# Two layers of linear attention and MLP on one core: the key weights in four loads, the last store on another queue, and new instruction orders

## The chip, the core and the metric

The kernel runs on one core of a Trainium2 chip. A core has five engines that run side by side, each through its own list of instructions in order: TensorE (PE in the profile; its weight loads are PEld), VectorE (DVE), ScalarE (ACT), GpSimd (POOL) and SyncE (SP). They meet through semaphores. DMAs are issued by an engine's sequencer (here SP, ScalarE and GpSimd) and move data while the engines work. The metric is the device time of one execution in microseconds; lower is better.

## What is computed

```python
def _A_ref(x, wqkv, wo):                      # linear attention, 32 heads of 16
    qkv = (x @ wqkv) ...                      # 2048 tokens, 512 -> 3 * 512
    phi = lambda t: jnp.where(t > 0, t + 1, jnp.exp(t)) + 1e-6
    pq, pk = phi(q), phi(k)
    kv = jnp.einsum("bhsd,bhse->bhde", pk, v)
    z = jnp.einsum("bhsd->bhd", pk)
    num = jnp.einsum("bhqd,bhde->bhqe", pq, kv)
    den = jnp.einsum("bhqd,bhd->bhq", pq, z)[..., None] + 1e-6
    return (num / den) ... @ wo

def _B_ref(x, w1, b1, w2, b2):                # MLP, 512 -> 1792 -> 512
    y = _layernorm(x, axis=-1)
    h = _gelu(jnp.einsum("bsd,df->bsf", y, w1) + b1)
    return jnp.einsum("bsf,fd->bsd", h, w2) + b2

x = A_x
x = x + _A_ref(_layernorm(x, axis=-1), A_wqkv, A_wo)
x = x + _B_ref(_layernorm(x, axis=-1), B_w1, B_b1, B_w2, B_b2)
x = x + _A_ref(_layernorm(x, axis=-1), A_wqkv, A_wo)
x = x + _B_ref(_layernorm(x, axis=-1), B_w1, B_b1, B_w2, B_b2)
```

Inputs and output are bf16; x has 2048 tokens of 512.

## The kernel before, in words

**Tiling.** The 2048 tokens are 16 tiles of 128 (st 0 to 15), four to a chunk (c 0 to 3). L is the layer, 0 or 1. Weights stay on the chip.

**The order is written out by hand.** `build_kernel` lists every operation with its engine, what it reads and writes, and the buffers it takes. `CONF["ORDER"]` gives, for each engine, the names of its operations in the order in which they run; `CONF["PLACES"]` the buffer slot of each tile; `CONF["WAY"]` which engine or method does an operation that several could do; `CONF["LOADS"]` the first loads, each with name, queue, tensor, chunk, first and last part, and what it is issued behind. Semaphore waits follow from these (`assign_waits`). No engine leaves its order, so an operation whose input is late holds up all that stands behind it on its engine.

**The start.** The loads are x0 (token tile 0 of chunk 0, 128 KB), x1 (tiles 1 to 3, 384 KB), wk0 and wk1 (key weights, parts 0 and 1, then 2 and 3, of four parts of the contraction, 256 KB each), xc1, xc2, xc3 (the other chunks of x, 512 KB each) and wq (query weights, 512 KB). Each tile is normalised: `stats` and `aggr` (L772, L774), `veps` (variance plus epsilon, L779), `pow` (L781, GpSimd), `norm` (L800 on DVE or L795 on ScalarE). The first two tiles are also centred only (`cen`, L786), so that their keys need not wait for the scale. The keys need the tokens transposed: tiles 0 to 3 by TensorE (`PTC`, `PTA0`, L822) with a copy by ScalarE (`tc`, L832); all others, and tiles 0 and 1 for the queries, by a DMA transpose on SP (`TA`, L809). `K0_st` (L876) are the four matmuls of a tile's keys, into one bank; `K0_0` is in two pieces, a (parts 2 and 3) and b (parts 0 and 1). `phi` follows: `exp` (L844) and `relu` (L855) on ScalarE, `min` (L857 or L848) and `phi` (L861 or L850) on DVE or GpSimd. Then `G` (keys by normalised tokens, L968, L997), `Q` (queries, L893, and L906 for chunk 0 of layer 0) and `Z` (sums of keys, L951). TensorE runs `warm` matmuls on constants (L746) until its first real input is there.

**Between the parts of a layer.** G is copied (`cpg`, L984 on DVE, L981 on ScalarE), `KV` (L1018) makes the value product, `kvm` (L1037, DVE) masks it, `M` (L1041) multiplies it by wo, and `cpm` copies the result into `gtb` (`cpm0_2` on DVE, L984; the other three on ScalarE, L981). `WO0_0_0` to `WO0_0_3` (L1107), one piece for each column of `gtb`, make the first tile's attention output. The denominators of chunks 1 to 3 are done by token: `pz` (L1061), `red` (L1064), `den`, `rec`, `pr` (L1073), then a DMA transpose on SP (`TP`, L1077).

**The MLP.** `W1` (L1137) with `gelu` (L1142), `W2` (L1174) with a residual add `RB` (L1180; in the last layer L1184, into a bf16 tile), `b2` (L1123) adds the bias ahead of it. `TB` are the DMA transposes of its normalised tokens. In the last layer each tile is stored by SP (`OD`, L1186).

**The end.** The last tile, 15, is done in two pieces: 384 columns (h0) and 128 columns (h1), each with its own matmuls (L1160), add (`RB1_15_0`, `RB1_15_1`, L1166) and store (`OD15_0`, `OD15_1`, L1168), both on SP. Tile 10 is the one before it on TensorE. SP's last orders are OD8, OD9, OD15_0, OD10, OD15_1; DVE's are RB1_9, RB1_8, RB1_15_0, RB1_10, RB1_15_1. SP waits for all stores at the end.

**attn_z.** It adds up the keys: in layer 0 by matmul with ones for each chunk (`Z0_c`); in layer 1 by adding tiles into `zacc` (`za`, DVE or GpSimd, L923) for the first three chunks, turned into sums by `ZH`, and by matmul for the fourth.

Of the kernel before, what the change touches and what calls it, by code (L numbers as in the profile page):

```python
# [1345 lines left out]
```

## Time and profile before

| what | value |
|---|---|
| median of 3 runs | 324.53 us (324.09 to 324.61) |
| the profiled execution | 324.26 us |
| its span, first to last instruction | 323.0 us |
| busy time of PE / DVE / ACT / POOL | 318.4 / 216.9 / 189.8 / 145.6 us |
| matmuls | 1703 |
| first real matmul (PTC0), first key matmul | 4.65, 5.81 us |
| last matmul ends (modelled) | 320.44 us |

The loads and first transposes, by issue and landing:

| load | queue | issued at (us) | landed at (us) |
|---|---|---|---|
| x0 | SP | 0.80 | 3.21 |
| x1 | SP | 1.25 | 4.33 |
| wk1 | ACT | 1.49 | 5.67 |
| wk0 | SP | 1.71 | 6.03 |
| xc1 | ACT | 3.23 | 7.42 |
| TA0_0 | SP | 5.54 | 8.04 |
| xc3 | SP | 6.89 | 10.55 |
| wq | SP | 7.50 | 11.97 |
| TA0_1 | SP | 9.00 | 12.61 |
| xc2 | SP | 10.24 | 14.50 |
| TA0_4 | SP | 11.80 | 14.99 |

A busy share near 100% on TensorE says that it is never long without an instruction, not that it runs at its best. Matmuls overlap, so the distance from one start to the next tells what a matmul costs in a row; the recorded duration (379 ns on average for 512 columns) is its whole passage. The busy shares of the span, in 40 slices:

```profile
PE   7999999999999999999999999999999999999996
DVE  6988799998886763027378999999868872101003
ACT  5898656696640628667782377888735333653320
POOL 6674598784427433303634215967835273000000
```

Each digit is the busy share of one slice in tenths. TensorE's row has two slices that are not 9, the first and the last.

### The profile page before, as it was taken

What the parts mean: (1) busy time and instruction counts of PE and PEld (TensorE: products, weight loads), DVE (VectorE), ACT (ScalarE), POOL (GpSimd) and SP (SyncE); (2) the same over time, 40 slices, a digit from 0 to 9 for tenths busy, and PEclk for the clock granted to TensorE, in tenths of its full rate; (3) what the DMA queues carried; (4) which work ended last, traced back from release to release, by engine and by line L of the source; (5) the groups of instructions that cost most, each with busy time, mean ns of one, the idle gap of its engine ahead of it and who ended that gap; (6) DMA issues with size and microseconds to landing.
All of it is one profiled execution on the core that took longest, in us unless ns stands there. A gap on an engine that the chain in (4) does not pass through costs nothing.

```text
span 323.0 us, 4748 instructions
## 1 busy us (share of the span) xinstructions
PE 318.4 (99%) x1703; PEld 157.5 (49%) x1703; DVE 216.9 (67%) x528; ACT 189.8 (59%) x324; POOL 145.6 (45%) x217
## 2 busy tenths in 40 slices
PE   7999999999999999999999999999999999999996
PEld 3444544666445444444444444558644444444443
DVE  6988799998886763027378999999868872101003
ACT  5898656696640628667782377888735333653320
POOL 6674598784427433303634215967835273000000
DMA  6843792332212413011101300132034222201002
GB/s 211 244 87 79 253 334 54 63 81 36 49 32 35 81 32 67 17 31 37 34 3 30 51 16 0 35 62 57 19 79 89 59 65 67 49 0 35 16 32 65
DMA packets 52323, 21.68 MB, mean 67 GB/s; under 512 B 47500, under 2 KB 50828, under 8 KB 52300
## 3 DMA queue, kind: packets, MB, share of 16 engines
q1 hardware_dynamic: 50828, 15.88, 22.7%
q0 software_dynamic: 1056, 4.72, 4.4%
q10 hardware_dynamic: 416, 0.79, 0.7%
q8 instruction: 13, 0.21, 0.3%
q14 instruction: 10, 0.08, 0.1%
...
## 4 chain that ended last, share of the span: by engine, by line
PE 92%; DVE 3%; POOL 2%; ACT 1%; DMA 1%; issue 0%
PE ps L1137 30%; PE ps L1174 29%; PE ps L876 9%; PE ps L1107 8%; PE ps L893 5%; PE ps L997 4%; PE ps L906 2%; PE ps L968 2%; DMA t<-in_A_x_dram 1%; POOL lr L1061 1%; POOL t L1092 1%; PE ps L1160 1%; PE ps L951 1%; POOL w L725 1%; DVE rd L1064 0%; DVE eb L848 0%
## 5 line engine op out<-in xcount | busy, mean ns | idle before, releaser
L1142 ACT ACTIVATE gT<-ps,b1c 128x512 bf16<-128x512 f32 (+1 forms) x140 | 76.8, 601 | 62.4 <-PE ps L1137 61.8
L1137 PE MATMUL ps<-t,w 128*128 128x512 bf16 (+1 forms) x560 | 102.7, 336 | 0.0
L1174 PE MATMUL ps<-w,gT 128*128 128x512 bf16 x434 | 98.2, 379 | 0.0
L1137 PEld LDWEIGHTS ps<-t,w 128*128 128x128 bf16 x560 | 54.8, 98 | 44.3 <-ACT gT L1142 0.4
L1174 PEld LDWEIGHTS ps<-w,gT 128*128 128x128 bf16 x434 | 42.5, 98 | 49.9
L844 ACT ACTIVATE eb<-ps 128x512 bf16<-128x512 f32 x62 | 36.1, 602 | 25.9 <-PE ps L876 10.9
L781 POOL TENSOR_TENSOR rstd<-veps,neghalf 128x1 f32<-128x1 f32 x64 | 38.1, 607 | 15.4 <-DVE veps L779 13.1
L1184 DVE TENSOR_TENSOR yb<-ps,xsb 128x512 bf16<-128x512 f32 x15 | 10.2, 685 | 43.9 <-PE ps L1174 43.9
L772 DVE BATCH_NORM_STATS2 stats<-xsb 128x6 f32<-128x512 f32 x48 | 32.2, 678 | 0.1
L1107 PE MATMUL ps<-gtb,t 128*128 128x512 bf16 x128 | 31.6, 379 | 0.4 <-DVE gtb L984 0.4
L876 PE MATMUL ps<-wqkv,t 128*128 128x512 bf16 x128 | 31.1, 379 | 0.6 <-ACT t L832 0.6
L795 ACT ACTIVATE yb<-xsb,nmr,rstd 128x512 bf16<-128x512 f32 x21 | 17.0, 815 | 20.0 <-POOL nmr L792 19.8
L855 ACT ACTIVATE rb<-ps 128x512 bf16<-128x512 f32 x43 | 25.3, 600 | 3.1 <-PE ps L893 2.1
L779 POOL TENSOR_SCALAR veps<-mv 128x1 f32<-128x1 f32 x36 | 10.6, 295 | 36.0 <-DVE mv L774 30.8
L1061 POOL TENSOR_TENSOR lr<-t,zrow 128x512 f32<-128x512 bf16 x17 | 20.1, 1182 | 10.7 <-DVE t L850 4.9
L893 PE MATMUL ps<-wqkv,t 128*128 128x512 bf16 x96 | 24.1, 379 | 0.0
L1123 POOL TENSOR_TENSOR xsb<-xsb,b2b 128x512 f32<-128x512 f32 x17 | 19.9, 1181 | 4.9 <-DVE yb L800 4.7
L1180 DVE TENSOR_TENSOR xsb<-ps,xsb 128x512 f32<-128x512 f32 x16 | 10.9, 688 | 15.6 <-PE ps L1174 15.5
L800 DVE TENSOR_SCALAR yb<-xsb,mv,rstd 128x512 bf16<-128x512 f32 x27 | 14.4, 533 | 9.7 <-POOL rstd L781 9.5
L1073 POOL TENSOR_TENSOR t<-t,rr 128x512 bf16<-128x512 bf16 x14 | 14.9, 1070 | 12.1 <-DVE rr L1069 10.9
L1107 PEld LDWEIGHTS ps<-gtb,t 128*128 128x128 bf16 x128 | 12.5, 98 | 15.1 <-DVE gtb L984 0.9
L876 PEld LDWEIGHTS ps<-wqkv,t 128*128 128x128 bf16 x128 | 12.2, 98 | 15.0 <-ACT t L832 1.0
(100 smaller groups left out, 364.7 us busy)
## 6 DMA issues: line engine op xcount, KB each, us to landing
...
t<-yb SPq DMA_TRANSPOSE x62, 2.5
...
```

Of the source, the lines that this page charges most:

```text
L772: G.op("dve", lambda e: e.bn_stats(stats[:, s.slot, :], src()), 620, reads=src_keys, writes=[k + "s"], tiles=[s, *src_tiles], name=f"stats ...
L781: G.op("pool", lambda e: e.tensor_tensor(rstd[:, s.slot:s.slot + 1], veps[:, s.slot:s.slot + 1], neghalf[:], op=ALU.pow), 570, reads=[k + ...
L844: G.op("act", lambda e: e.activation(eb[:, et.slot, :], bank(bt), ACT.Exp, scale=by()), 478, reads=[src_key, *more_keys], writes=[f"e{tag} ...
L855: G.op("act", lambda e: e.activation(rb[:, rt.slot, :], bank(bt), ACT.Relu, scale=by()), 478, reads=[src_key, *more_keys], writes=[f"r{tag ...
L876: ins = e.matmul(bank(b), lhsT=yTa(yT)[:, dt, k * P:(k + 1) * P], rhs=wqkv[:, dt, D:2 * D], start=(i == 0 and n == 0), stop=(i == len(part ...
L893: ins = e.matmul(bank(b), lhsT=yTa(yT)[:, dt, k * P:(k + 1) * P], rhs=wqkv[:, dt, 0:D], start=(dt == 0), stop=(dt == DT - 1))
L1061: lambda e, r=r, tok=tok: e.tensor_tensor(lr[:, r.slot, :], tok(), zrow[:], op=ALU.mult), 1150 if on_pool else 600,
L1107: ins = e.matmul(bank(wb), lhsT=yTa(pq)[:, kt, k * P:(k + 1) * P], rhs=gtb[:, kt, :], start=(kt == 0), stop=(kt == DT - 1))
L1123: G.op("pool" if on_pool else "dve", lambda e: e.tensor_tensor(xsb[:, st, :], xsb[:, st, :], b2b[:], op=ALU.add), 1120 if on_pool else 600 ...
L1137: ins = e.matmul(bank(b, n), lhsT=w1[:, dt, ft * P:(ft + 1) * P], rhs=yTa(yT)[:, dt, k0 * P:k1 * P], start=(dt == 0), stop=(dt == DT - 1))
L1142: G.op("act", lambda e, ft=ft, b=b, k0=k0, k1=k1, n=n: e.activation(gT[:, g.slot, ft * 512 + k0 * P:ft * 512 + k1 * P], bank(b, n), ACT.Ge ...
L1174: ins = e.matmul(bank(b), lhsT=gT[:, g.slot, ft * 512 + k * P:ft * 512 + (k + 1) * P], rhs=w2[:, ft, :], start=(ft == 0), stop=(ft == FT - 1))
```

## The change

**Loads.** The key weights come in four loads of one part each, 128 KB: wkb (part 2) and wkd (part 3) on ScalarE's queue, wka (part 0) and wkc (part 1) on SP's. xc1 moves from ScalarE's queue to SP's. SP now issues xc1, wq and xc3 ahead of the first transpose, TA0_0.

**The first tile's keys.** K0_0 is in four pieces, in the order of parts 2, 0, 3, 1, each reading its own load; PTC1 stands between the second and the third.

**The end.** RB1_10 and OD10 stand ahead of RB1_15_0 and OD15_0. OD15_1 is issued by ScalarE.

**Orders.** All five orders are new. By place, 359 of 387 entries of TensorE's differ, 489 of 528 of DVE's, 191 of 310 of ScalarE's, 201 of 213 of GpSimd's and 100 of 112 of SP's. 435 of 705 tiles have another slot. 43 small operations change between DVE and GpSimd: 22 go to DVE, 21 to GpSimd. The set switches of ScalarE's table stay 14.

**attn_z** is rewritten so that the chunks of layer 0 that are added by `za`-like operations could be listed under a setting `zc0`. The setting is in neither configuration, so layer 0 goes by matmul as before, and layer 1 as before.

```diff
-    LOADS=[['x0', 'sp', 'x', 0, 0, 1, ''], ['x1', 'sp', 'x', 0, 1, 4, ''], ['wk0', 'sp', 'wk', 0, 0, 2, ''], ['wk1', 'act', 'wk', 0, 2, 4, 'ones'], ['xc1', 'act', 'x', 1, 0, 4, 'x0'], ['xc3', 'sp', 'x', 3, 0, 4, ''], ['wq', 'sp', 'wq', 0, 0, 4, ''], ['xc2', 'sp', 'x', 2, 0, 4, '']],
+    LOADS=[['x0', 'sp', 'x', 0, 0, 1, ''], ['x1', 'sp', 'x', 0, 1, 4, ''], ['wkb', 'act', 'wk', 0, 2, 3, 'ones'], ['wka', 'sp', 'wk', 0, 0, 1, ''], ['wkd', 'act', 'wk', 0, 3, 4, ''], ['wkc', 'sp', 'wk', 0, 1, 2, ''], ['xc1', 'sp', 'x', 1, 0, 4, 'x0'], ['wq', 'sp', 'wq', 0, 0, 4, ''], ['xc3', 'sp', 'x', 3, 0, 4, ''], ['xc2', 'sp', 'x', 2, 0, 4, '']],
         "sp":
-            "x0 x1 wk0 TA0_0 xc3 wq TA0_1 xc2 TA0_4 TA0_5 TA0_7 TA0_6 TA0_13 TA0_12 TA0_14 TA0_15 TA0_8 TA0_10 TA0_9 TA0_11 "
...
-            "OD11 OD12 OD8 OD9 OD15_0 OD10 OD15_1",
+            "x0 x1 wka wkc xc1 wq xc3 TA0_0 TA0_1 xc2 TA0_5 TA0_4 TA0_7 TA0_6 TA0_13 TA0_14 TA0_15 TA0_12 TA0_8 TA0_10 TA0_9 "
...
+            "OD11 OD12 OD8 OD9 OD10 OD15_0",
         "pe":
-            "warm0 warm8 warm4 warm7 warm5 PTC0 warm3 warm2 warm6 warm1 K0_0a K0_0b PTC1 PTA0_2 K0_1 PTA0_3 K0_2 G0_0_0 K0_3 "
-            "G0_1_0 Q0_0_2 Q0_0_1 Q0_0_0 K0_4 Q0_1_0 K0_5 G0_2_0 G0_3_0 G0_4_0 K0_7 Q0_1_3 K0_6 Z0_0 G0_5_0 K0_13 Q0_1_2 "
...
+            "warm0 warm8 warm2 warm6 PTC0 warm1 warm7 warm5 warm4 warm3 K0_0a K0_0b PTC1 K0_0c K0_0d PTA0_2 K0_1 PTA0_3 K0_2 "
+            "K0_3 G0_0_0 G0_1_0 Q0_0_2 Q0_0_1 Q0_0_0 K0_5 G0_2_0 K0_4 Z0_0 G0_3_0 Q0_1_0 K0_7 Q0_1_3 K0_6 G0_4_0 G0_5_0 "
...
         "act":
-            "wk1 xc1 sumA0_3 tcC0 sqA0_3 expk0_0 tcC1 tcA0_2 reluk0_0 expk0_1 tcA0_3 reluk0_1 expk0_2 reluk0_2 reluk0_3 "
...
+            "wkb wkd sumA0_3 tcC0 sqA0_3 tcC1 reluk0_0 tcA0_2 expk0_0 tcA0_3 expk0_1 reluk0_1 reluk0_3 expk0_2 reluk0_2 "
...
+            "gelu1_2_10_0 OD15_1",
         "dve":
-            "ones statsA0_0 aggrA0_0 vepsA0_0 cenA0_0 statsA0_2 normA0_0 aggrA0_2 statsA0_1 vepsA0_2 aggrA0_1 cenA0_1 "
-            "vepsA0_1 normA0_2 statsA0_4 normA0_3 mink0_0 normA0_1 aggrA0_4 phik0_0 statsA0_7 mink0_1 statsA0_5 phik0_1 "
...
-            "pr0_0_2 pz0_1_3 red0_1_3 den0_1_3 rec0_1_3 cpg0_2 cpg0_3 cpg0_0 cpg0_1 red0_1_0 red0_1_1 kvm0_2 den0_1_1 kvm0_0 "
-            "rec0_1_1 kvm0_1 kvm0_3 den0_1_0 minq0_2_0 red0_1_2 cpm0_2 phiq0_2_0 rec0_1_0 den0_1_2 RA0_0 rec0_1_2 statsB0_0 "
...
-            "RB1_5 b21_9 RB1_4 b21_11 RB1_7 RB1_13 RB1_12 RB1_14 RB1_11 RB1_9 RB1_8 RB1_15_0 RB1_10 RB1_15_1",
+            "ones statsA0_0 aggrA0_0 cenA0_0 statsA0_2 statsA0_1 aggrA0_2 aggrA0_1 cenA0_1 normA0_0 vepsA0_1 normA0_2 "
...
+            "kvm0_3 cpm0_2 red0_1_2 rec0_1_1 den0_1_0 minq0_2_0 phiq0_2_0 rec0_1_0 den0_1_2 RA0_0 rec0_1_2 statsB0_0 RA0_1 "
...
+            "b21_10 RB1_5 b21_9 RB1_4 b21_11 RB1_7 RB1_13 RB1_12 RB1_14 RB1_11 RB1_9 RB1_8 RB1_10 RB1_15_0 RB1_15_1",
         "pool":
-            "powA0_9 powA0_11 nmrA0_11 b1z phik0_14 wv phik0_8 wo w1_0 w1_1 phiq0_1_1 w2_0 w2_1 pr0_0_0 pz0_1_0 pr0_0_3 "
...
+            "nmrA0_10 vepsA0_9 powA0_9 nmrA0_11 phik0_14 eps6 wv wo phik0_8 w1_0 w1_1 w2_0 w2_1 phiq0_1_1 pr0_0_0 pz0_1_0 "
...
             halves = eng(f"ks{st}") if L == 0 else None
-            parts = [(2, 3), (0, 1)] if halves else [tuple(range(DT))]
+            parts = [tuple(int(x) for x in p) for p in halves.split("|")] if halves else [tuple(range(DT))]
...
-                     writes=[f"k{L}_{st}"], tiles=[b, yT], name=f"K{L}_{st}" + "ab"[i] * (len(parts) > 1), lat=MM_DRAIN, n=len(part))
+                     writes=[f"k{L}_{st}"], tiles=[b, yT], name=f"K{L}_{st}" + "abcd"[i] * (len(parts) > 1), lat=MM_DRAIN, n=len(part))
...
+            by_sum = [int(v) for v in (eng("zc0") or "").split()] if L == 0 else list(range(NC - 1))
...
+            if c in by_sum:
+                for k in range(4):
+                    st = 4 * c + k
+                    if L not in zfirst:
+                        zfirst[L] = (pks[k], f"pk{L}_{st}", True)
+                        continue
...
+                if L == 1 and c == by_sum[-1]:
+                    fold(False)
                 return
...
-                    dma("sp", lambda e, cs=cs: e.dma_start(rows(out_dram, c)[:, k, cs], yb[:, ot.slot, cs]), [f"od{st}_{h}"],
+                    dma("act" if h else "sp", lambda e, cs=cs: e.dma_start(rows(out_dram, c)[:, k, cs], yb[:, ot.slot, cs]), [f"od{st}_{h}"],
```

`fold` holds what layer 1 did in place before: the sum in `zacc` is split into two bf16 parts and multiplied by ones (`ZH`). In `WAY`, `ks0` goes from "1" to "2|0|3|1".

More of the change, by code (lines that the diff above doesn't have):

```diff
@@ L954, in attn_z @@
             G.op("pe", fn, 400, reads=[f"pk{L}_{4 * c + k}" for k in range(4)] + ["onesm"], writes=[f"zc{L}_{c}"], tiles=[b, *pks], name=f"Z{L}_{c}", lat=MM_DRAIN, n=16)
-            if c == 0:
-                G.op("dve", lambda e: e.tensor_scalar(zs[:], bank(b)[:, 0:DT], 1.0, None, op0=ALU.mult), 130, reads=[f"zc{L}_{c}"],
-                     writes=["zs"], tiles=[b], name=f"zs{L}_{c}", lat=40)
-            else:
-                G.op("dve", lambda e: e.tensor_tensor(zs[:], bank(b)[:, 0:DT], zs[:], op=ALU.add), 130, reads=[f"zc{L}_{c}", "zs"],
-                     writes=["zs"], tiles=[b], name=f"zs{L}_{c}", lat=40)
+            total(b, f"zc{L}_{c}", f"zs{L}_{c}", bool(L) or c != min(v for v in range(NC) if v not in by_sum))
+            if L == 0 and by_sum and c == max(v for v in range(NC) if v not in by_sum):
+                fold(True)
         def attn_g_held(L, st, k, y, ykey, pk, gb):
@@ L1266, in build_kernel @@
                 if L == 0:
-                    if c == 0:
-                        pk0s = pks
                     attn_z(1, c, pks)
```

44 lines of the change are left out of this document (24 added, 20 removed), and 464 rows, old and new, of tables (ORDER, PLACES, WAY).

## The prediction

> **What bounds the kernel now.** I read the busy time by stage first, cut where the matmul stream changes: columns are the stretch, its length, then busy time and instructions of PE, PEld, DVE, ACT and POOL, the clock, the DMA share and GB/s.
>
> ```profile
> 0.00:8.10 8.10, 6.42 (x32) 2.77 (x32) 5.06 (x16) 4.55 (x9) 4.96 (x16) 1.00 0.65 212
> 8.10:12.60 4.50, 4.50 (x24) 2.09 (x24) 4.43 (x15) 4.34 (x9) 2.41 (x6) 1.00 1.01 316
> 12.60:50.00 37.40, 37.40 (x242) 18.13 (x242) 33.30 (x88) 28.88 (x51) 25.90 (x43) 1.00 0.65 180
> 50.00:206.00 156.00, 155.63 (x811) 76.56 (x809) 113.77 (x277) 96.44 (x161) 71.96 (x99) 1.00 0.21 39
> 206.00:317.00 111.00, 111.00 (x571) 55.72 (x570) 58.77 (x134) 55.54 (x97) 40.35 (x57) 1.00 0.21 47
> 317.00:323.00 6.00, 3.44 (x30) 2.23 (x28) 1.55 (x4) 0.00 (x0) 0.00 (x0) 1.00 0.27 87
> ```
>
> TensorE is full from 8.10 to 317. Matmuls end late in the record, so I also looked at their starts: from 8.10 on a 512-column matmul starts every 0.216 us (the chain of waits has 0.86 for each group of four). Only one gap over 0.2 us breaks this, at WO0_0_2. The change adds no matmul: K0_0 is the same four in four pieces. So only three places can give time back (before 8.10, at that gap, after the last matmul); anywhere else it can only be lost. Second, the first 10 us of the timeline (start, duration, engine, line):
>
> ```profile
> 5.09 0.60 ACT L832 ACTIVATE t<-ps 128x512 bf16<-128x512 bf16 x1
> 5.81 1.02 PE L876 MATMUL ps<-wqkv,t 128*128 128x512 bf16 x4 [0.31 <-ACT t L832]
> 6.43 0.35 DVE L786 TENSOR_SCALAR yb<-t,mv 128x512 bf16<-128x512 bf16 x1
> 7.45 1.07 ACT L832 ACTIVATE t<-ps 128x512 bf16<-128x512 bf16 x2
> 8.10 1.04 PE L876 MATMUL ps<-wqkv,t 128*128 128x512 bf16 x4 [0.30 <-ACT t L832]
> 9.76 0.59 ACT L832 ACTIVATE t<-ps 128x512 bf16<-128x512 bf16 x1
> ```
>
> K0_0 starts at 5.81, when ScalarE's copy tcC0 (5.09 to 5.69) ends: it waits for its tokens, not for its weights. K0_1 starts at 8.10, after tcC1 at 7.45, which stood behind expk0_0 and behind DVE's centring of token 1 (6.43). Third, the gap and the end:
>
> ```profile
> 49.34 1.32 DVE L848 TENSOR_SCALAR eb<-eb 128x512 bf16<-128x512 bf16 x1
> 50.58 0.67 DVE L1064 TENSOR_REDUCE rd<-lr 128x32 f32<-128x512 f32 x1
> 50.95 0.59 PE L1107 MATMUL ps<-gtb,t 128*128 128x512 bf16 x2
> 51.17 0.67 DVE L984 TENSOR_SCALAR gtb<-ps 128x512 bf16<-128x512 f32 x1
> 51.91 0.82 PE L1107 MATMUL ps<-gtb,t 128*128 128x512 bf16 x3 [0.37 <-DVE gtb L984]
> ...
> 317.22 3.22 PE L1160 MATMUL ps<-w,gT 128*128 128x384 bf16 x28
> 319.70 0.56 DVE L1166 TENSOR_TENSOR yb<-ps,xsb 128x384 bf16<-128x384 f32 x1 [2.50 <-PE ps L1160]
> 320.17 0.68 DVE L1184 TENSOR_TENSOR yb<-ps,xsb 128x512 bf16<-128x512 f32 x1
> 320.28 0.33 SPq L1168 DMA_DIRECT2D out_dram<-yb  x1
> 320.77 0.28 DVE L1166 TENSOR_TENSOR yb<-ps,xsb 128x128 bf16<-128x128 f32 x1
> 320.88 0.33 SPq L1186 DMA_DIRECT2D out_dram<-yb  x1
> 321.26 0.43 SPq L1168 DMA_DIRECT2D out_dram<-yb  x1
> ```
>
> Copy cpm0_2 (L984) had its input at 48.6 but stood behind minq0_2_0 and red0_1_2 until 51.17. At the end DVE idles 2.50 us with RB1_10 ready (its matmul ended at 317.38), then does it between the two pieces of tile 15, which delays the last piece and puts three stores in SP's queue.
>
> **Tail.** RB1_10 moves into the idle: 317.43 to 318.11; its store follows OD9 (issued by 318.04) and lands near 320. RB1_15_0 and its store stay (320.28). RB1_15_1 no longer waits for DVE; the last matmul ends at 317.22 + 3.22 = 320.44, so it runs 320.48 to 320.76 in place of 320.77 to 321.05. ScalarE, idle since 309.0, issues at 320.79 in place of SP's 321.26: 0.47 earlier, of which 0.28 is DVE and 0.19 SP's queue. SP's two tile-15 stores landed 1.7 to 1.8 us after their issue; the span ended at 323.0, so the new end is 322.55. No row has a store by ScalarE. Nearest: its 512 KB load landed in 4.2 us, SP's in 4.0, so up to 0.2 worse; ScalarE's shortest issue (0.35) beside SP's 0.43 gives 0.08 better. **-0.45, bounds -0.55 to -0.25.** A rule speaks on this term: the Trainium skill (DMA: Bandwidth & Descriptors, Issuing engines are not separate DMA queues) says a second issuing engine saves only the sequencer's time. By that rule the move to ScalarE is worth only 0.19, and the rest is DVE's order; the sum would be the same.
>
> **Head.** The four loads move the same 512 KB. wk1 landed at 5.67 and wk0 at 6.03; K0_0's third matmul started at 6.24. So the weights held nothing, and the split by itself is worth 0; its one more issue (0.48 on ScalarE, behind the first at 1.49) ends by 2.5, under ScalarE's wait until 4.36. If that cover were gone it would delay sumA0_3 by 0.48. The order gives the time. DVE loses vepsA0_0 (0.15), vepsA0_2 (0.13) and normA0_0 (0.40, with overlap 0.32) ahead of cenA0_1, which goes from 6.43 to 5.95. PTC1 follows at 6.3 in place of 6.84, K0_0c and K0_0d then end near 7.1 (0.3 later than now), tcC1 starts at 6.75 in place of 7.45, now ahead of expk0_0, and K0_1, behind PTA0_2, at 7.53: 0.57 earlier. Next on ScalarE, by starts 0.5 to 0.6 apart: reluk0_0 7.24, tcA0_2 7.84, expk0_0 8.33, tcA0_3 about 8.95 to 9.55. tcA0_3 also waits for normA0_3 (8.05, unchanged, since statsA0_5 before it needs xc1, landing at 7.42). K0_2 starts at 8.7, K0_3 at 9.6, G0_0_0 at 10.5, G0_1_0 at 11.3, Q0_0_2 at 12.15 in place of 12.65. Its other input, TA0_1, is issued near 8.95 (9.00 now). On SP it is now behind xc1, wq, xc3 and TA0_0. Loads in a row land about 1.4 us apart (wk0 6.03, xc1 7.42; xc3 10.55, wq 11.97): xc1 7.4, wq 8.8, xc3 10.2, then TA0_0 and, a further 0.64 behind (12.61 after 11.97), TA0_1 near 11.5. That just holds. Best -0.55; nothing where a later input eats it: minq0_0_2 now stands ahead of phik0_2, and from Q0_0_2 to G0_2_0 PE has four groups, 3.46 us, for matmul 1.03, exp 0.60, min 0.29, stats and aggregate 0.85, phi 0.42 and the hops, 3.3. I take **-0.40, bounds -0.55 to +0.30**, the latter if ScalarE's new order costs K0_2 half an ACTIVATE more.
>
> **Middle.** cpm0_2 moves right behind kvm0_3 (48.83 to 49.10), so it ends at 49.7, before its slot at 51.38; the gap was 51.91 - 50.95 - 2 x 0.216 = 0.53. M0_2 and M0_0 also lost 0.16 to kvm0_2, which stood behind a reduction that waited for GpSimd; w2's two issues (0.9 each) leave that GpSimd chain for its idle time from 37 to 39. So up to -0.69. What is late next: 359 of 387 places in PE's order, 489 of 528 in DVE's and most of the others change, and PE waits in order. Many present margins are thin (W1 groups start 0.2 us after the gelu that frees their bank, Z1_3 0.22 after phik1_15, D1_0_0 0.13 after zb1). I followed the groups that move forward most. K1_15 goes up 1.7 us, but TA1_15 is now third of four, not last, and its norm loses 2.6 us of queue. WO1_15_0 goes up 5.8 us, to 240.2, while TP1_3_3 landed at 244.1; it leaves OD3 and TP1_2_1 behind and should land near 238.3. These hold by 2 us. The 43 operations that trade DVE for GpSimd (vepsX 0.14 against 0.29, pr 0.70 against 1.10, pz 0.74 against 1.18) hide under engines idle 33% and 55%; without that cover each costs some 0.4. New small waits of 0.1 to 0.2 in two or three places, like those now at M0_2 and M0_0, take back 0.34. **-0.35, bounds -0.69 to +0.80** (a wait of the size of the present gap twice, with some small ones). The sums-of-keys code (attn_z) is rewritten, but its setting is absent, so it issues the same operations: 0.
>
> **Sum.** -0.45 - 0.40 - 0.35 = -1.20. The profiled run was 324.26, its span 323.0 and 1.2 around it; 324.26 - 1.20 = 323.06. The median shown, 324.53, stands 0.27 above that run, so the forecast is 323.3, its own range 322.5 to 323.9.
>
> **Rivals.** (a) Only the tail counts: the gains ahead are eaten by inputs that do not move, and the loads do not do what the change says of them. For: K0_0 ends 0.3 later, G0_2_0's margin is 0.2. Against: cpm0_2 moves by 2 us. 324.53 - 0.45 = 324.1. (b) New waits of 0.80 in the middle: 324.53 - 0.45 - 0.40 + 0.80 = 324.5. (c) **Slower**: TA0_1 lands late, because SP's queue now carries 1.5 MB ahead of both transposes. The worst spacing of landings in a row is xc1 to xc3, 3.13. At that pace wq lands at 10.55, xc3 at 13.68, TA0_1 at 14.96; Q0_0_2 waits until 15.0, and the head costs 2.35: 324.53 + 2.35 - 0.80 = 326.1. It decides from a landing of 13.4, where it has eaten the 0.80 of tail and middle. Against: that worst spacing had TA0_0 and an idle queue in it. (d) The clock rises one step later. The warm-up matmuls start 0.427 apart until 3.77, later ones 0.216. PTC0 now stands ahead of five warm-up blocks, not four. Were half rate kept to 7.6, K0_0 would take 0.85 more and the head would be +0.45: 324.2. The Trainium skill (TensorE: Matmul & The Clock Gate, The HAM clock gate) calls its window free-running, so this can befall any run; the three runs shown, within 0.5 us, show no such jump.
>
> **Chances.** Forecast 55%, (a) 17, (b) 12, (c) 12, (d) 4. Under 0.2% (0.65 us) this kernel's runs can't tell from no change. Faster than 323.88: 48 of the forecast's 55, 7 of (a), 2 of (b): 57. Slower than 325.18: 10 of (c), 2 of (b) and 2 of the forecast, where an unseen wait is larger than its bound: 14. Same: 29. The range reaches from 322.5, all three parts at their best, to 325.2, past (a), (b) and (d), leaving most of (c) out.
>
> **What would show it.** Tail: L1184 before both L1166 rows, the last store on ScalarE's queue, 2.3 us between the last matmul's end and the span's. Head: K0_1 near 7.5, Q0_0_2 (first L906) near 12.15. Middle: no L984 wait near 51; PE's idle below 0.4 us from 13 to 317. Wrong: L906 held by a transpose past 12.7, or TensorE waits over 0.5 us between 13 and 317.

## The result and the profile after

The changed kernel takes 322.90 us (median of 5 runs, 322.65 to 323.47) beside 324.53 us for the kernel before in the same session: a ratio of the means of 0.9956, 95% interval 0.9941 to 0.9970. A second sample, in another session, gave 323.93 (12 runs, 322.51 to 325.75) beside 324.84 (35 runs, 324.07 to 325.73): 0.9970, interval 0.9953 to 0.9986. By the medians it is faster by 0.9 to 1.6 us. The profiled execution took 323.10 us with a span of 321.85, where before had 324.26 and 323.02.

The busy time by stage of the changed kernel first, cut at the same places (from 206 on one us earlier); columns as in the prediction: the stretch, its length, busy time and instructions of PE, PEld, DVE, ACT and POOL, the clock, the DMA share and GB/s.

```profile
0.00:8.10 8.10, 6.68 (x34) 2.83 (x34) 4.38 (x13) 4.31 (x9) 5.32 (x17) 1.00 0.74 258
8.10:12.60 4.50, 4.03 (x22) 1.68 (x21) 4.40 (x13) 4.13 (x9) 2.17 (x5) 1.00 0.87 197
12.60:50.00 37.40, 37.40 (x243) 18.27 (x242) 32.59 (x90) 29.26 (x52) 26.19 (x44) 1.00 0.64 185
50.00:206.00 156.00, 156.00 (x813) 76.93 (x811) 114.60 (x276) 96.20 (x163) 75.40 (x102) 1.00 0.19 39
206.00:316.00 110.00, 110.00 (x567) 55.26 (x565) 59.88 (x140) 55.38 (x96) 36.42 (x51) 1.00 0.20 47
316.00:321.90 5.90, 3.92 (x33) 2.43 (x30) 2.22 (x5) 0.00 (x0) 0.00 (x0) 1.00 0.27 89
```

Two things are new. TensorE now loses 0.47 between 8.10 and 12.60, where it was full, and it is full from 50 to 206, where 0.37 was missing. The first of these in the timeline (start, duration, engine, line, operation, and in brackets the idle time before it and what ended that):

```profile
5.23 0.58 ACT L835 ACTIVATE t<-ps 128x512 bf16<-128x512 bf16 x1
6.14 0.35 DVE L789 TENSOR_SCALAR yb<-t,mv 128x512 bf16<-128x512 bf16 x1
6.98 0.60 ACT L835 ACTIVATE t<-ps 128x512 bf16<-128x512 bf16 x1 [0.47 <-PE ps L825]
7.67 1.03 PE L879 MATMUL ps<-wqkv,t 128*128 128x512 bf16 x4
8.09 0.69 DVE L775 BATCH_NORM_STATS2 stats<-t 128x6 f32<-128x512 bf16 x1 [0.72 <-DMA t<-in_A_x_dram]
8.70 0.40 DVE L803 TENSOR_SCALAR yb<-t,stats,rstd 128x512 bf16<-128x512 bf16 x1
9.16 0.40 PE L825 MATMUL ps<-idp,yb 128*128 128x128 bf16 x4 [0.47 <-DVE yb L803]
9.39 1.89 PE L879 MATMUL ps<-wqkv,t 128*128 128x512 bf16 x8
12.85 0.38 PE L909 MATMUL ps<-t,wqkv 128*128 128x512 bf16 x1
```

K0_1 (7.67) is 0.43 earlier than before. Then DVE idles 0.72 for xc1, which landed at 8.07 and not at 7.42. statsA0_5 (8.09) stands ahead of normA0_3 (8.70), and PTA0_3 (9.16) waits for that. Q0_0_2, the first L909, starts at 12.85, 0.20 later than before.

The middle and the end of the same timeline:

```profile
48.37 0.81 PE L1057 MATMUL ps<-wo,kvb 128*128 128x512 bf16 x3
48.79 0.69 DVE L1000 TENSOR_SCALAR gtb<-ps 128x512 bf16<-128x512 f32 x1
50.96 1.89 PE L1123 MATMUL ps<-gtb,t 128*128 128x512 bf16 x8
...
316.70 3.22 PE L1176 MATMUL ps<-w,gT 128*128 128x384 bf16 x28
316.90 0.69 DVE L1200 TENSOR_TENSOR yb<-ps,xsb 128x512 bf16<-128x512 f32 x1 [0.22 <-PE ps L1190]
319.18 0.56 DVE L1182 TENSOR_TENSOR yb<-ps,xsb 128x384 bf16<-128x384 f32 x1 [1.58 <-PE ps L1176]
319.76 0.33 SPq L1184 DMA_DIRECT2D out_dram<-yb  x1
319.96 0.29 DVE L1182 TENSOR_TENSOR yb<-ps,xsb 128x128 bf16<-128x128 f32 x1 [0.22 <-PE ps L1176]
320.28 0.35 ACTq L1184 DMA_DIRECT2D out_dram<-yb  x1
```

cpm0_2 (L1000) runs at 48.79 and is done at 49.48; the output projection (L1123) runs its eight matmuls without a gap, where before had 0.53 inside them. At the end RB1_10 (L1200) lies in DVE's idle time, the last add starts 0.04 us after the last matmul's end (319.92), and its store is issued 0.03 us after the add.

Cut at two events that both kernels have, the span divides like this (us, from the two profiled executions):

| part | before | after | difference | predicted |
|---|---|---|---|---|
| start to Q0_0_2 | 12.65 | 12.85 | +0.20 | -0.40 |
| Q0_0_2 to the last matmul's end | 307.79 | 307.07 | -0.72 | -0.35 |
| last matmul's end to the span's end | 2.58 | 1.93 | -0.65 | -0.45 |
| span | 323.02 | 321.85 | -1.17 | -1.20 |

The sum came out within 0.03, but only because the head's miss of 0.60 was made up by the other two parts. These are single executions: the kernel's middle varies from one to the next, as the experiments show.

### The profile page after: what moved, and what is told of

It is laid out like the page before. It is cut to its first block, busy times and chain, and to the rows that moved or that the text cites. A ratio compares the mean times of both kernels' runs of the same rounds, so it can differ in the third digit from the quotient of the medians.

```text
span 321.9 us, 4748 instructions
## 1 busy us (share of the span) xinstructions
PE 318.0 (99%) x1703; PEld 157.4 (49%) x1703; DVE 218.1 (68%) x529; ACT 189.3 (59%) x324; POOL 145.5 (45%) x216
## 4 chain that ended last, share of the span: by engine, by line
PE 97%; DMA 2%; DVE 0%; issue 0%
PE ps L1153 30%; PE ps L1190 29%; PE ps L1123 9%; PE ps L879 8%; PE ps L896 6%; PE ps L984 4%; PE ps L1013 4%; DMA t<-in_A_x_dram 2%; PE ps L909 2%; PE ps L1176 1%; PE ps L970 1%; PE ps L1034 1%; PE ps L1057 1%; PE ps L1100 1%; DVE stats L775 0%; PE ps L1048 0%
## 5 line engine op out<-in xcount | busy, mean ns | idle before, releaser
L784 POOL TENSOR_TENSOR rstd<-veps,neghalf 128x1 f32<-128x1 f32 x64 | 39.0, 625 | 41.1 <-DVE veps L782 38.9
L847 ACT ACTIVATE eb<-ps 128x512 bf16<-128x512 f32 x62 | 35.4, 606 | 19.3 <-PE ps L896 7.3
L1200 DVE TENSOR_TENSOR yb<-ps,xsb 128x512 bf16<-128x512 f32 x15 | 10.2, 688 | 41.4 <-PE ps L1190 41.4
L1123 PE MATMUL ps<-gtb,t 128*128 128x512 bf16 x128 | 31.4, 379 | 0.0
L858 ACT ACTIVATE rb<-ps 128x512 bf16<-128x512 f32 x43 | 25.3, 607 | 5.8 <-PE ps L879 5.8
L896 PE MATMUL ps<-wqkv,t 128*128 128x512 bf16 x96 | 24.1, 379 | 0.0
L1089 POOL TENSOR_TENSOR t<-t,rr 128x512 bf16<-128x512 bf16 x18 | 19.3, 1072 | 9.0 <-DVE rr L1085 6.4
L782 POOL TENSOR_SCALAR veps<-mv 128x1 f32<-128x1 f32 x35 | 8.2, 236 | 32.7 <-DVE mv L777 31.3
L1139 POOL TENSOR_TENSOR xsb<-xsb,b2b 128x512 f32<-128x512 f32 x17 | 21.4, 1267 | 3.0 <-DVE yb L803 2.9
L1077 POOL TENSOR_TENSOR lr<-t,zrow 128x512 f32<-128x512 bf16 x14 | 16.5, 1179 | 7.3 <-ACT zrow L997 4.5
L1123 PEld LDWEIGHTS ps<-gtb,t 128*128 128x128 bf16 x128 | 12.5, 98 | 14.5
```

The costliest lines, as they stand in the source:

```text
L784: G.op("pool", lambda e: e.tensor_tensor(rstd[:, s.slot:s.slot + 1], veps[:, s.slot:s.slot + 1], neghalf[:], op=ALU.pow), 570, reads=[k + ...
L847: G.op("act", lambda e: e.activation(eb[:, et.slot, :], bank(bt), ACT.Exp, scale=by()), 478, reads=[src_key, *more_keys], writes=[f"e{tag} ...
L858: G.op("act", lambda e: e.activation(rb[:, rt.slot, :], bank(bt), ACT.Relu, scale=by()), 478, reads=[src_key, *more_keys], writes=[f"r{tag ...
L896: ins = e.matmul(bank(b), lhsT=yTa(yT)[:, dt, k * P:(k + 1) * P], rhs=wqkv[:, dt, 0:D], start=(dt == 0), stop=(dt == DT - 1))
L1089: lambda e, d=d, tok=tok, heads=heads: e.tensor_tensor(heads(tok()), heads(tok()), rr[:, d.slot, :].unsqueeze(2).broadcast_to([P, H, DH]), ...
L1123: ins = e.matmul(bank(wb), lhsT=yTa(pq)[:, kt, k * P:(k + 1) * P], rhs=gtb[:, kt, :], start=(kt == 0), stop=(kt == DT - 1))
```

## The experiments

Eleven edited kernels and the changed kernel once more, in three sessions. The ratios come from 5 to 12 runs of each kernel and 5 to 35 of the kernel before; where the parts of the span are compared, they come from the one profiled execution of each kernel, cut as in the table above. In the diffs a line starts with the engine whose order is edited.

| kernel | ratio to before (95% interval) | x1, xc1 landed | K0_1, PTA0_3 | start to Q0_0_2 | to last matmul's end | to span's end |
|---|---|---|---|---|---|---|
| before | | 4.33, 7.42 | 8.10, 8.97 | 12.65 | 307.79 | 2.58 |
| changed | 0.9956 (0.9941-0.9970) | 4.58, 8.07 | 7.67, 9.16 | 12.85 | 307.07 | 1.93 |
| tail_sp | 0.9966 (0.9951-0.9981) | 4.71, 7.87 | 7.80, 8.96 | 12.64 | 307.07 | 1.91 |
| tail_order | 0.9996 (0.9981-1.0011) | 5.75, 8.08 | 8.84, 9.70 | 13.54 | 307.06 | 2.70 |
| cpm_late | 1.0000 (0.9983-1.0016) | 4.64, 7.74 | 7.73, 8.83 | 12.52 | 307.72 | 1.93 |
| norm3_first | 0.9954 (0.9939-0.9970) | 4.52, 7.47 | 7.61, 8.47 | 12.39 | 307.38 | 1.93 |
| two_loads | 0.9947 (0.9927-0.9966) | 4.66, 8.17 | 8.14, 9.26 | 12.95 | 307.21 | 1.93 |
| xc1_act | 1.0060 (1.0038-1.0081) | 4.65, 10.76 | 7.73, 11.85 | 17.23 | 307.06 | 1.93 |
| before_tail | 0.9978 (0.9964-0.9991) | 4.45, 7.45 | 8.35, 9.23 | 12.93 | 308.30 | 1.92 |
| before_cpm | 1.0003 (0.9987-1.0020) | 4.41, 7.58 | 8.25, 9.12 | 12.86 | 308.20 | 2.57 |
| after_again | 0.9970 (0.9953-0.9986) | 5.37, 7.81 | 8.46, 9.32 | 13.16 | 307.11 | 1.93 |
| ta5_first | 0.9969 (0.9955-0.9982) | 4.54, 7.64 | 7.70, 8.57 | 12.43 | 307.54 | 1.93 |
| ta54_first | 0.9996 (0.9976-1.0017) | 4.55, 7.63 | 7.95, 8.82 | 12.68 | 307.68 | 1.94 |
| ta5_sp | 0.9968 (0.9953-0.9983) | 4.68, 7.85 | 7.80, 8.67 | 12.56 | 307.50 | 1.90 |

An interval is some 0.5 us wide on either side, so the parts tell more than the ratios, and a part is trusted where the line that makes it is in the trace. The expectations below take 1.98 for the changed kernel's end; cut as in the table it is 1.93.

### The tail: whose queue, or whose order?

**tail_sp**: the changed kernel with its last store back on SP, behind OD15_0.

```diff
 emit of OD15
-dma("act" if h else "sp", ...)
+dma("sp", ...)
-act: ... gelu1_2_10_0 OD15_1
+act: ... gelu1_2_10_0
-sp:  ... OD9 OD10 OD15_0
+sp:  ... OD9 OD10 OD15_0 OD15_1
```

> The changed kernel with the last store (OD15_1) issued by SP again, the rest as changed. Theory (the tail gained from DVE's order and, apart from it, from SP's queue): the last add ends at the same place, 0.6 us after the last matmul starts to end; SP issues OD15_1 when it is through with OD15_0, and the time from the last matmul's end (modelled) to the span's end grows from 1.98 to about 2.1 to 2.2. Rival (ScalarE's queue itself lands a small store sooner or later than SP's): issue to landing of OD15_1, 1.53 us on ScalarE, comes out as 1.53 on SP too if the queue does not matter, and as 1.72 as in the kernel before if it does. Head and middle unchanged; time within 0.2 us of the changed kernel's.

Last matmul's end to span's end was 1.91, beside 1.93 with ScalarE, and not the 2.1 to 2.2 that the theory expected. The end of its timeline has both stores in one group of SP. The group begins at 319.55; its second issue, the last store's, is at 320.07, 0.03 behind the last add's end:

```profile
319.55 0.85 SPq L1184 DMA_DIRECT2D out_dram<-yb  x2
319.75 0.29 DVE L1182 TENSOR_TENSOR yb<-ps,xsb 128x128 bf16<-128x128 f32 x1 [0.22 <-PE ps L1176]
```

The store landed 1.50 us after its issue here and 1.53 from ScalarE. With OD10 out of the way SP is through with OD15_0 at 319.88 and free when the last add ends. ScalarE's part in the change is worth nothing that this shows.

**tail_order**: the changed kernel with RB1_10 and OD10 back between the two pieces of tile 15, the last store still by ScalarE.

```diff
-dve: ... RB1_8 RB1_10 RB1_15_0 RB1_15_1
+dve: ... RB1_8 RB1_15_0 RB1_10 RB1_15_1
-sp:  ... OD9 OD10 OD15_0
+sp:  ... OD9 OD15_0 OD10
```

> The changed kernel with RB1_15_0 ahead of RB1_10 on DVE and OD15_0 ahead of OD10 on SP, as before; OD15_1 stays on ScalarE. Theory (DVE's order is most of the tail's gain): RB1_15_1 starts 0.28 to 0.3 us later, OD15_1 is issued 0.3 later, the time from the last matmul's end to the span's end is 2.25 to 2.35 in place of 1.98. Rival (the store's landing, not the add, sets the end, through stores that share the DMA engines): OD10, now issued late beside OD15_1, makes the span end 0.6 later, 2.6 after the last matmul, whoever issues OD15_1.

The end took 2.70, more than the 2.58 of the kernel before: the rival's 2.6 and not the theory's 2.25 to 2.35. Its timeline:

```profile
319.86 0.56 DVE L1182 TENSOR_TENSOR yb<-ps,xsb 128x384 bf16<-128x384 f32 x1 [2.50 <-PE ps L1176]
320.33 0.68 DVE L1200 TENSOR_TENSOR yb<-ps,xsb 128x512 bf16<-128x512 f32 x1
320.93 0.28 DVE L1182 TENSOR_TENSOR yb<-ps,xsb 128x128 bf16<-128x128 f32 x1
321.04 0.33 SPq L1202 DMA_DIRECT2D out_dram<-yb  x1
321.24 0.35 ACTq L1184 DMA_DIRECT2D out_dram<-yb  x1
```

ScalarE does issue at once, 0.03 us behind the add. But the store landed 2.02 us after its issue, where the same store took 1.53 in the changed kernel and 1.72 in before. What is different is OD10, 128 KB, issued 0.20 us earlier on the other queue. So a free queue was no help while the larger store was on its way: 0.18 was saved in issuing and 0.30 lost in landing (one profile). The Trainium skill (DMA: Bandwidth & Descriptors, Issuing engines are not separate DMA queues) says that a second issuing engine saves only the sequencer's time of issuing. These two runs agree: where SP's sequencer is free the other engine gains nothing (1.93 against 1.91), and where it is busy the gain is the 0.18 of the issue and none of the landing.

**before_tail**: the kernel before with the change's end alone, its three edits of the orders and the store by ScalarE.

> The kernel before with the reordered end alone: RB1_10 and OD10 ahead of RB1_15_0 and OD15_0, OD15_1 issued by ScalarE. Theory (the end is a part of its own): from the last matmul's end to the span's end 1.9 to 2.0 in place of 2.58, the time 0.55 to 0.65 less than the kernel before's. Rival (the gain needs the other orders, or the landing of a store is as long as before): 2.2 or more, 0.3 or less.

The end went from 2.58 to 1.92, and the ratio is 0.9978 (0.9964 to 0.9991): the tail alone gains, and by itself accounts for what the ratio shows. The profiled span, 323.16, was yet no shorter than before's 323.02, for reasons outside the edit. Q0_0_2 was 0.28 later, and TensorE lost 1.05 us at the first W1 matmul, which the waits of TensorE name:

```profile
PE ps L1137 <- DMA t<-yb: 0.9, 1, 0.9
```

This is transpose TB0_1, which landed at 61.72 here, 61.31 in before_cpm and 60.22 in before. In the changed order, with b2's load earlier in SP's order, it landed at 59.3 to 60.6 (leaving out xc1_act, where everything is 4.4 later). One landing that varies by 1.5 us, against a slot near 61, is a risk of the kernel before. No profile of the changed order waits there: it landed 0.95 to 0.97 ahead of its slot in ten of them, 0.30 in ta54_first. How often it strikes was not counted.

On the other side, the gap of 0.53 at WO0_0_2, on which the prediction's middle rests, is not in this profile, though the order up to there is that of the kernel before. The difference is minq0_2_0 (L848). In before it took 1.32 at 49.34, beside a GpSimd operation that began at the same time:

```profile
49.34 1.17 POOL L1092 TENSOR_TENSOR t<-t,lr 128x512 bf16<-128x512 bf16 x1
```

Here it began 0.01 ahead of that operation and took 0.28, so cpm0_2 (L984) ran in time and the projection (L1107) without a gap:

```profile
49.61 0.28 DVE L848 TENSOR_SCALAR eb<-eb 128x512 bf16<-128x512 bf16 x1
49.62 1.29 POOL L1092 TENSOR_TENSOR t<-t,lr 128x512 bf16<-128x512 bf16 x1
50.41 0.68 DVE L984 TENSOR_SCALAR gtb<-ps 128x512 bf16<-128x512 f32 x1
51.22 1.89 PE L1107 MATMUL ps<-gtb,t 128*128 128x512 bf16 x7
```

So the order leaves cpm0_2 open to this delay, and one of two executions had it.

### The middle: is it cpm0_2?

**cpm_late**: the changed kernel with cpm0_2 back behind its neighbours.

```diff
-dve: kvm0_3 cpm0_2 red0_1_2 rec0_1_1 den0_1_0 minq0_2_0 phiq0_2_0
+dve: kvm0_3 rec0_1_1 den0_1_0 minq0_2_0 red0_1_2 cpm0_2 phiq0_2_0
```

> The changed kernel with cpm0_2 put back behind rec0_1_1, den0_1_0, minq0_2_0 and red0_1_2 on DVE, as before. Theory (the gap at WO0_0_2 closed because cpm0_2 moved): the gap between WO0_0_1 and WO0_0_2 comes back, 0.4 to 0.6 us, TensorE's idle time from 13 to 317 goes from 0 to that, and the span grows by as much. Rival (the gap closed because GpSimd's chain is earlier, w2's issues having left it): no gap, or under 0.1 us, the span as it is.

The middle grew by 0.65 (307.07 to 307.72), and by the ratio (1.0000) the whole gain was gone. The profiled execution is the fastest of the twelve, 323.41 beside a median of 325.05, so the parts may show less than the ratio. minq0_2_0 took 0.28 in it. The timeline has the 0.65 at one place:

```profile
49.68 0.68 DVE L1000 TENSOR_SCALAR gtb<-ps 128x512 bf16<-128x512 f32 x1
50.41 1.04 PE L896 MATMUL ps<-wqkv,t 128*128 128x512 bf16 x4 [0.49 <-DVE gtb L1000]
51.28 1.03 PE L1123 MATMUL ps<-gtb,t 128*128 128x512 bf16 x4
```

The size is that of the old gap, but the waiter is another one. It is not the output projection that reads cpm0_2 (L1123 runs on without a gap) but the Q group ahead of it (L896), which needs the bank that cpm0_2 empties. By starts the group came 0.865 behind the one before it in place of 0.216.

**before_cpm**: the kernel before with only cpm0_2 moved forward.

```diff
-dve: kvm0_1 kvm0_3 den0_1_0 minq0_2_0 red0_1_2 cpm0_2 phiq0_2_0
+dve: kvm0_1 kvm0_3 cpm0_2 den0_1_0 minq0_2_0 red0_1_2 phiq0_2_0
```

> The kernel before with cpm0_2 alone moved right behind kvm0_3 on DVE. Theory: the gap of 0.53 between WO0_0_1 and WO0_0_2 goes and nothing takes its place; the small ones at M0_2 and M0_0 (0.16) stay, since they come from red0_1_1; 0.4 to 0.55 us less. Rival (red0_1_2, now later by 0.7, or minq0_2_0 takes the place of cpm0_2): a new wait of 0.3 or more at WO0_1_0 or behind it.

No gain: ratio 1.0003 (0.9987 to 1.0020), and the middle took 308.20, more than before's 307.79. The gap at WO0_0_2 is gone, as it is without the move in before_tail. Others stand in its place: 0.49 before K0_4 for TA0_4, which is ahead of the edit and not due to it (landed 15.81, behind xc2 at 15.26), and two behind the edit, 0.27 ahead of 54.48 and 0.19 ahead of 58.13. The last line names what ended the idle time ahead of the weight load:

```profile
50.30 0.92 DVE L1067 TENSOR_SCALAR rd<-rd 128x32 f32<-128x32 f32 x1
51.14 1.21 DVE L848 TENSOR_SCALAR eb<-eb 128x512 bf16<-128x512 bf16 x1
53.75 0.67 DVE L1112 TENSOR_TENSOR xsb<-ps,t 128x512 f32<-128x512 f32 x1
54.47 1.41 PEld L1107 LDWEIGHTS ps<-gtb,t 128*128 128x128 bf16 x8 [0.59 <-DVE xsb L1112]
```

The projection waits for DVE's adds (L1112), which empty its banks, and DVE is late for them: den0_1_0 (L1067) took 0.92 and minq0_2_0 1.21 beside two GpSimd operations, where in before_tail they took 0.39 and 0.28. Of the 0.53, 0.46 came back as new waits, and with the 0.49 for TA0_4 that makes 0.42 more, near the 0.41 by which the middle grew. So in the changed order cpm0_2's place is needed (cpm_late), and moved alone it gained nothing here (before_cpm). Whether the edit itself or the two long DVE operations cost the 0.46 is not separated: the time of these operations differs between executions of one order.

### The head: why was it not 0.40 earlier?

**norm3_first**: the changed kernel with normA0_3 ahead of statsA0_5, so that it doesn't wait for xc1.

```diff
-dve: statsA0_5 normA0_3 aggrA0_5 normA0_1
+dve: normA0_3 statsA0_5 aggrA0_5 normA0_1
```

> The changed kernel with normA0_3 one place forward on DVE, ahead of statsA0_5. Theory (the head lost what it could have gained because normA0_3 stood behind statsA0_5, which waited for the load xc1 until 8.07): normA0_3 runs at about 7.9, PTA0_3 at 8.5 in place of 9.16, TensorE's idle of 0.47 before PTA0_3 goes, Q0_0_2 starts at 12.2 to 12.4 in place of 12.85, and the span shrinks by 0.4 to 0.6. Rival 1 (ScalarE's order is the bound behind it): K0_3 or G0_1_0 then waits as long, Q0_0_2 at 12.7 or later, the span within 0.15. Rival 2 (transposes of the next tiles are the bound): Q0_0_2 is early but K0_5 waits for TA0_5 until 15.1, so that the span shrinks by 0.3 at most.

PTA0_3 came at 8.47 and Q0_0_2 at 12.39, 0.46 earlier than in the changed kernel: the stand behind xc1 was what held the head. But the middle lost 0.31 of it again (307.38):

```profile
15.30 0.81 PE L879 MATMUL ps<-wqkv,t 128*128 128x512 bf16 x3 [0.15 <-ACT yb L798]
```

That is K0_5. The line names ScalarE, but the last of its inputs was transpose TA0_5, landed at 15.16, right behind xc2 (14.59) on SP. In the changed kernel K0_5 starts at 15.44 and TA0_5 landed at 15.14, so at most 0.30 us could be gained before the next landing decides; K0_5 came 0.14 earlier and the span was 0.15 shorter. This is the second rival of the expectation.

**two_loads**: the changed kernel with the key weights in two loads, as before.

```diff
-LOADS: wkb act 2-3, wka sp 0-1, wkd act 3-4, wkc sp 1-2
+LOADS: wk0 sp 0-2, wk1 act 2-4
-sp:  x0 x1 wka wkc xc1
+sp:  x0 x1 wk0 xc1
-act: wkb wkd sumA0_3
+act: wk1 sumA0_3
```

> The changed kernel with the key weights in two loads as before (parts 0 and 1 on SP, 2 and 3 on ScalarE), K0_0 still in four pieces, all orders as changed. Theory (the split is worth nothing): K0_0's pieces still start behind tcC0 and PTC1, not behind a load; K0_1 within 0.1 us of 7.67 once x1's landing is allowed for; time as the changed kernel's. Rival 1 (the split helps): the last weights land after 6.2 and K0_0c or K0_0d waits for them. Rival 2 (the four loads are what makes x1 and xc1 land later, 4.5 to 4.7 and 7.5 to 8.1 in the changed order, 4.33 and 7.42 before): x1 lands by 4.4 and xc1 by 7.5.

Here the weights do hold K0_0, twice, as the first rival has it:

```profile
6.26 0.38 PE L879 MATMUL ps<-wqkv,t 128*128 128x512 bf16 x1 [0.28 <-DMA wqkv<-in_A_wqkv_dram]
6.84 0.39 PE L879 MATMUL ps<-wqkv,t 128*128 128x512 bf16 x1 [0.21 <-DMA wqkv<-in_A_wqkv_dram]
...
8.14 0.39 PE L879 MATMUL ps<-wqkv,t 128*128 128x512 bf16 x1
```

wk1 landed at 6.12 and wk0 at 6.80, and K0_1 came at 8.14, 0.47 later than with four loads. Yet Q0_0_2 was only 0.10 later (12.95), since PTA0_3 waits for normA0_3 and xc1 all the same, and the ratio, 0.9947 (0.9927 to 0.9966), overlaps the changed kernel's. x1 (4.66) and xc1 (8.17) were as late as with four loads, so in this profile the number of loads is not what delays them.

**xc1_act**: the changed kernel with xc1 issued by ScalarE, behind its two weight loads; the kernel before has it there behind one. SP, without it, issues wq and xc3 a microsecond earlier, at 2.65 and 3.12.

```diff
-LOADS: xc1 sp
+LOADS: xc1 act
-sp:  x0 x1 wka wkc xc1 wq xc3
+sp:  x0 x1 wka wkc wq xc3
-act: wkb wkd sumA0_3
+act: wkb wkd xc1 sumA0_3
```

> The changed kernel with xc1 on ScalarE's queue again, behind wkd; wq and xc3 on SP right behind wkc, without a wait for x0. Theory (xc1 is late, 7.5 to 8.1, since SP's queue serves it behind five loads): xc1 lands at 7.4 or earlier, statsA0_5 and normA0_3 follow, PTA0_3 at 8.5 to 8.6, and K0_5 still waits for TA0_5 near 15.1, so the span is 0.1 to 0.3 shorter at most. Rival (all loads share the same bandwidth, so wq and xc3, now issued at 2.6 ahead of xc1, push it back): xc1 lands at 9 to 10, PTA0_3 at 10 or later, the span 0.5 to 1.5 longer.

Slower, ratio 1.0060 (1.0038 to 1.0081). xc1 landed at 10.76, after wq (9.58) and just ahead of xc3 (10.93). It was issued at 3.22, as early as in the changed kernel (3.24), but now behind these two loads of 512 KB instead of ahead of them. That is the rival of the expectation. The chain is the same as in the changed kernel, only longer: statsA0_5, normA0_3, PTA0_3.

```profile
10.79 0.69 DVE L775 BATCH_NORM_STATS2 stats<-t 128x6 f32<-128x512 bf16 x1 [3.34 <-DMA t<-in_A_x_dram]
11.85 0.40 PE L825 MATMUL ps<-idp,yb 128*128 128x128 bf16 x4 [3.09 <-DVE yb L803]
```

xc1 came 2.69 us later than in the changed kernel, PTA0_3 2.69 and Q0_0_2 4.38. The remaining 1.69 are TensorE's clock, shown by its column (0.57) in the stages from 8.1 to 16:

```profile
8.10:12.00 3.90, 0.81 (x7) 0.25 (x5) 1.21 (x4) 1.19 (x3) 0.34 (x2) 1.00 0.71 191
12.00:16.00 4.00, 4.00 (x14) 1.56 (x14) 3.49 (x11) 2.32 (x5) 2.13 (x6) 0.57 0.50 122
```

TensorE had idled 3.09 us. The matmuls from 11.85 still start at the full rate; from 12.63 to 15.61 the 512-column ones start 0.427 apart, not 0.216. These seven steps, 0.211 longer each, and a part of the step on either side (0.11 and 0.10, where one record is missing) make the 1.69. So the chain from xc1 to Q0_0_2 is shown by a landing that moved, and the step that the prediction took for free is worth its full size.

### Can the head's gain be had after all?

**after_again**: the changed kernel, unedited, beside the next three.

> The changed kernel itself once more, beside the three others on one chip. Theory (its time hangs on when the first loads land): the same waits, PTA0_3 behind normA0_3 behind xc1; Q0_0_2 at 12.85 plus or minus what x1 and xc1 land later or sooner than 4.58 and 8.07; no TensorE wait behind that, 1.9 to 2.0 us from the last matmul's end to the span's end. Rival: a wait in the middle that one profile did not show.

The second sample of the result above. x1 landed at 5.37, and Q0_0_2 followed at 13.16; the middle and the end repeat within 0.04 (307.11, 1.93). So the head's size changes from one execution of the same kernel to the next.

**ta5_first**: norm3_first, and TA0_5 ahead of xc2 on SP.

```diff
-sp:  TA0_0 TA0_1 xc2 TA0_5 TA0_4
+sp:  TA0_0 TA0_1 TA0_5 xc2 TA0_4
```

> normA0_3 ahead of statsA0_5 on DVE, and on SP TA0_5 ahead of xc2 (then TA0_4). Theory (K0_5 waited for TA0_5, which landed 0.6 behind xc2 on the same queue): TA0_5 lands at 13.5 to 13.9, K0_5 follows Q0_0_0 without a wait, near 15.0 in place of 15.3, and the span is 0.3 shorter than with normA0_3 alone moved. Rival 1: K0_4 now waits for TA0_4 behind xc2, landing at 16.7 or later, and takes 0.1 to 0.5 back. Rival 2: statsA0_8, which needs xc2, holds up DVE and something behind 17 us waits.

TA0_5 landed at 13.58 and K0_5 ran at 15.02 without a wait. Then K0_4 waited for TA0_4, which landed at 17.06, behind xc2 at 16.43:

```profile
17.20 0.59 PE L879 MATMUL ps<-wqkv,t 128*128 128x512 bf16 x2 [0.28 <-DMA t<-yb]
```

By starts that cost 0.45, as the first rival has it. Q0_0_2 was at 12.43, the middle at 307.54: together 319.97, against the changed kernel's 319.92.

**ta54_first**: both transposes ahead of xc2 (sp: TA0_0 TA0_1 TA0_5 TA0_4 xc2).

> The same, with xc2 behind both TA0_5 and TA0_4. Theory: neither K0_5 nor K0_4 waits; xc2 lands at 17 to 17.7. Rival: statsA0_8 stands on DVE near 16.7 and waits for xc2 until then; what is behind it on DVE is up to 1 us later, and TensorE waits for a phi between 18 and 23 us, 0.2 to 0.8.

xc2 landed at 17.61, and DVE idled 1.05 us for it ahead of statsA0_8, which is the rival. TensorE then waits 0.35 ahead of 24.66, ended by DVE's phi (L853), and 0.24 ahead of 26.64, ended by ScalarE's relu (L858). Ratio 0.9996 (0.9976 to 1.0017), no gain that can be told from zero; the profiled span, 322.30, gives up 0.44 of the 1.17.

**ta5_sp**: ta5_first with tail_sp's end.

> The kernel with TA0_5 ahead of xc2, and OD15_1 on SP again. Theory (the last store gains nothing from ScalarE once OD10 is out of the way): from the last matmul's end to the span's end 1.9, not above 1.98 as with ScalarE. Rival: 2.1 or more.

The end took 1.90, as tail_sp's 1.91: SP as the issuer of the last store is as good a second time. The whole is no faster than the changed kernel (ratio 0.9968, 0.9953 to 0.9983).

No version beat the changed kernel by more than the intervals. The lowest profiled run, tail_sp at 322.86, and the lowest ratio, two_loads with 0.9947 (0.9927 to 0.9966), can't be told from it.

## Why the prediction came out

**The total** was forecast as 323.3 and measured as 322.90 and 323.93, and the span went down by 1.17 where the sum said 1.20. The terms were off by more than that, so that the sum comes so close is luck: the errors cancel.

**Tail, -0.45: right for DVE, wrong for ScalarE, 0.20 too small.** RB1_15_1 starts 0.04 after the last matmul, as predicted (it was 0.33: -0.29), and its issue follows by 0.03 in place of 0.21 (-0.18). The two make the 0.47 that the prediction had before its allowance for ScalarE. The rest is the landing, 1.53 in place of 1.72 (-0.19), which was assumed at the old 1.7 to 1.8: the store no longer travels close behind OD10's 128 KB. The bounds, -0.55 to -0.25, missed the -0.65. What the prediction put down to the move to ScalarE (0.19 of "SP's queue") is OD10's removal instead: tail_sp has it all with SP.

**Head, -0.40: wrong, +0.20 measured.** The step that failed is "normA0_3 (8.05, unchanged, since statsA0_5 before it needs xc1, landing at 7.42)". The dependence was seen, and the landing was carried over from a kernel that issues its loads in another order. In the ten profiles that issue it on SP behind the weights it landed at 7.47 to 8.17. K0_1 at 7.67 was near the predicted 7.53 (tcC1 at 6.98 for 6.75), but it had no effect behind PTA0_3, which came at 9.16. norm3_first shows that this link held it, and the profiles agree: in after, tail_sp, cpm_late and two_loads Q0_0_2 starts 4.77 to 4.78 behind xc1's landing, and in xc1_act 6.47, which is this and the clock's 1.69. norm3_first also shows that the predicted gain had a second limit, TA0_5 behind xc2, which was not followed: only TA0_1 was, and it landed at 11.98 for the predicted 11.5.

**"The weights held nothing": right for the one execution shown, too strong as a rule.** wk1 landed at 5.67 in before, and at 5.93 in before_tail and 6.12 in two_loads, where K0_0 waits for it. In two_loads the split would be worth 0.47 at K0_1, and normA0_3 hides it.

**Middle, -0.35: the place was right, its size was one execution's, and the allowance for new waits was not needed.** Both old gaps went (0.53 and 0.16) and nothing came in their place: after 9.4 no gap of TensorE over 0.04 us is left. 0.72 was gained, 0.03 beyond the best bound, and the 0.34 taken off for "new small waits" didn't come. But the 0.53 hung on minq0_2_0's 1.32 us, which the prediction read as the cost of standing behind it. In before_tail that operation took 0.28 and the gap is absent, so it was luck that the execution profiled had this gap, and that it had not the 1.05 for TB0_1. cpm_late shows that cpm0_2's place matters in the changed order (0.65), though through a bank and not through the projection's input. Each of the three profiles of the old order waits somewhere in its middle (0.53; 1.05; 0.49, 0.27 and 0.19), and the two of the unedited changed kernel nowhere by over 0.05 behind 11. What the change is worth there in a usual run is not settled. Head and middle are also not independent, as the sum has them: in norm3_first 0.46 gained ahead of Q0_0_2 cost 0.31 behind it.

**The rivals.** (a), the tail alone, gives 324.1, and the second sample (323.93) isn't far from that: its interval, 0.9953 to 0.9986, overlaps that of before_tail, 0.9964 to 0.9991. What speaks against it are the profiles, where the changed kernel's middle (307.07, 307.11) was shorter than in all three of the old order (307.79 to 308.30), and cpm_late, where 0.65 of it is lost again. (b), new waits of 0.80, did not come. (c) needed TA0_1 after 13.4; it came at 11.98. xc1_act showed that its kind was real: a load displaced by others costs more than the whole change gains. (d), the clock one step later, was not in the changed kernel's profile: K0_0's first pair of matmuls, at 5.86, takes 0.60 in all, as two at the higher rate do. It was in three others with the same start on TensorE: ta5_first, ta54_first and ta5_sp. Their warm-up matmuls of 256 columns still start 0.21 apart at 5.8, where the changed kernel's start 0.11 apart from 4.84. The second matmul of K0_0 starts 0.32 to 0.43 behind the first, not 0.23, and K0_1 came at 7.70 to 7.95, against 7.61 in norm3_first. The sign that the prediction gives for the rise, 0.427 until 3.77 and 0.216 after, compares matmuls of 512 columns with ones of 256: in before those start 0.21 apart until 4.20 and 0.11 apart from there. "The three runs shown, within 0.5 us" were too few to judge the spread: 35 runs of the same kernel reach from 324.07 to 325.73.

**What stays open.** The changed kernel's runs reach from 322.5 to 325.8. Two things behind it show. Where x1 lands late (5.37 in after_again, 5.75 in tail_order), Q0_0_2 starts 7.79 behind x1, which is then later than 4.78 behind xc1. And the slowest run of after_again, 325.75, has a mean granted clock of 0.995, as have the slowest of before_tail and tail_order, two of ta54_first and most of xc1_act; all other runs have 0.998 or more. What dropped the clock in the runs that weren't profiled isn't known. x1 landed at 4.33 to 4.45 in the three kernels with the old order of loads and at 4.52 to 5.75 in the eleven with the new one, where wq and xc3 are issued by 4.6 and not from 6.9 on. That the loads behind delay the load ahead is one reading, and no run isolates it: none issues wq and xc3 later and keeps all else. Against it, xc1_act issues them a microsecond earlier and x1 landed at 4.65.
